# Two attentions and two gated layers on one core: where the first four weight units are loaded and converted

## The chip, the cores and the metric

The kernel runs on one core of one Trainium2 chip. The metric is device time of one execution in microseconds (us), lower is better. The engines named below are TensorE (PE, with its weight loads shown as PEld), VectorE (DVE), ScalarE (ACT), GpSimd (POOL) and SyncE (SP, which here only issues DMAs).

## The reference, cut to what matters

Four batches of 576 tokens. Attention runs per batch with 8 heads of 64 columns: scores, a threshold at the row maximum minus `tau`, exponentials of what is above it, division by their sum, times `v`. The four results, side by side as 2304 rows of 512, then pass two layers of the same shape:

```python
h = x @ w_in                       # 512 -> 2048
g = h * clip(h + 3, 0, 6) / 6      # layer 1; layer 2: g = max(h, 0)**2
x = g @ w_out                      # 2048 -> 512
```

Activations are f32 in and out.

## The kernel before, in words

**Attention.** A *unit* is one pair of heads of one batch (16 units, `u0` to `u15`), and a unit has nine *jobs* of 128 query rows (four of head 0, one for both tails, four of head 1). Batches 0 and 1 are jobs 0 to 71. `attention()` is a generator, and one *attention step* is one pass of the loop in `run` (line 457): `scores` and `soft1` of job i, `soft2` of job i-1, the product with v (`av`) of job i-5 (`LAG`), a bit of preparation of the next unit, and on three of nine jobs a load of k, q or v. A job's chain is: score matmuls on PE (L289), row minimum on DVE (L299), exponential on ACT (L309), threshold and sum on DVE (L316), cast to f16 on ACT (L322), the remainder on POOL (L323, L324), a transpose by DMA from SP's queue (L326), and the `av` matmuls (L348). Tiles of the job that matter here: the f16 pair p16 of a job in batches 0 and 1 is taken by `new_w("o")` (L318), so it sits in one of the **four `wpo` buffers** (`N_W = 4`), which are the buffers of converted `w_out` units. It is held from L322 until its transpose has landed. The products of `av`, the transposed results (`finish`, L365) and the small broadcast matmuls of `all_max` (L117) share two PSUM buffers (`ps_a`).

**Weights.** The weights come as f64 words. A *weight unit* is 256 of the 2048 hidden columns of `w_in`, or hidden rows of `w_out`: 1 MB in HBM. `wseq` lists them in order of use; numbers 0, 1 are the first `w_in` pair (kind i), 2, 3 the first `w_out` pair (kind o), 4, 5 i, 6, 7 o, and so on, 32 for both layers of batches 0 and 1. `w_load` brings one in (L538, L541) into one of three raw buffers (`wd`, `NWD = 3`). `group_scale` needs both units of a pair: a reduction of each on DVE (L557), `all_max` on PE (L117), a few small DVE operations. `w_next` then converts one unit into an exact f16 pair: ACT (L624), DVE (L627 and L628 for units 0 to 3; for later ones ACT L632 and DVE L633), the cast on ACT (L635) into a `wpi` or `wpo` buffer, the remainder on POOL (L636), and a store of the pair to a scratch in HBM from SP's queue (L638), from which batches 2 and 3 read it later.

**The layers.** The matmuls of the layers come in *steps* of 24 matmuls of 288 columns: a hidden step (`hidden`, L702: one of 16 blocks of 128 hidden columns of one batch) with its gate (ACT L706, DVE L707, ACT L712, POOL L713), and an output step (`output`, L742: one of four blocks of output columns over four hidden blocks). Both take their PSUM from the three `ps_s` buffers, which the attention scores also use. Segments alternate between batch 0 and batch 1; the order of steps at the start is: hidden 0 to 3 of batch 0 (steps 0 to 3), the first hidden step of batch 1 (step 4), four output steps of batch 0 (5 to 8), the other three hidden steps of batch 1 (9 to 11), the first hidden step of the next group (12). A weight unit serves two hidden blocks: step 0 needs unit 0, step 2 unit 1, step 5 units 2 and 3 (all four blocks are summed), step 12 unit 4, step 18 unit 5, step 21 units 6 and 7. Step 4 needs x of batch 1, so all of jobs 36 to 71 and `split_x(1)`.

**The order.** It is written out by hand at the end of the kernel. `attn_to(n)` runs the attention up to step n. Before: attention alone to step 50, convert unit 0 (`want_w(0)`), to 54, unit 1, to 58, unit 2, to 62, unit 3, to 64; then the layers start. Each layer step yields twice, and `paced` runs attention steps between these half steps: steps 64 to 77 over half steps 0 to 8 (`ways`), then the attention of batch 2 over half steps 8 to 232. `tick` converts unit k ahead of layer step 4k - 12 (`LEAD_J`), so unit 4 at step 4, 5 at 8, 6 at 12, 7 at 16. `most` caps how far raw loads run ahead. All this is program order; the framework then plans each engine's own order of issue from it, ahead of time, and may put an instruction that is ready ahead of earlier ones that are not.

Of the kernel before, what the change touches and what calls it, by code (L numbers as in the profile page):

```python
# [21 lines left out]

LAG = 5
LOADS = (2, 4, 6)
FIRST_W = (50, 54, 58, 62)
FIRST_LD = 64
AHEAD = 8
PRE = 6
LEAD_J = 12
LEAD = 8  # L30
# [7 lines left out]
def attention_moe_moe_kernel(  # L38
# [12 lines left out]
    nc = tc.nc  # L51
# [333 lines left out]
    def split_scaled(b, src, s):  # L385
        for c in range(NC):
            new_x(b, c)
            nc.scalar.activation(out=xh[b][c], in_=src[c], func=AF.Copy, scale=s)
            nc.vector.scalar_tensor_tensor(out=xl[b][c], in0=src[c], scalar=s, in1=xh[b][c], op0=ALU.mult, op1=ALU.subtract)

    def split_x(b):
        s = st.tile([P, 1], F32, name="sx", bufs=2)
        e = xe[b] = st.tile([P, 1], F32, name="ex", bufs=4)
        nc.vector.tensor_reduce(out=s, in_=vscs[b], axis=AX.X, op=ALU.min)
        nc.vector.reciprocal(out=e, in_=s)
        src = []
        for c in range(NC):
            if b < 2:
                src.append(x_st[b][:, c, :])
            else:  # L400
                t = me.tile([P, S], F32, name="xr", bufs=2)
                nc.sync.dma_start(out=t, in_=x_st[b][c])
                src.append(t)
        split_scaled(b, src, s)
# [94 lines left out]
    wseq = []  # L499
# [20 lines left out]
    w_hl = {}  # L520
    n_ld = [0]
    n_sp = [0]
    most = [len(FIRST_W)]
    w16s = {}
    scaled = {}

    def new_w(kind):
        return wt.tile([P, 2, UW], F16, tag=f"wp{kind}", name=f"wp{kind}", bufs=N_W)

    def w_load():  # L530

        k = n_ld[0]
        src, kind, u, layer, b = wseq[k]
        n_ld[0] += 1
        t = wt.tile([P, UW, 2], I32, name="wd", bufs=NWD)
        if kind == "i":
            v64 = src[:, u * UF:(u + 1) * UF].rearrange("(c p) f -> p c f", p=P).bitcast(I32)
            nc.sync.dma_start(out=t.rearrange("p (c f) t -> p c (f t)", c=NC), in_=v64)  # L538
        else:
            v64 = src[u * UF:(u + 1) * UF, :].rearrange("(a p) e -> p a e", p=P).bitcast(I32)  # L540
            nc.sync.dma_start(out=t.rearrange("p (a e) t -> p a (e t)", a=UC), in_=v64)  # L541
        w_raw[k] = t
# [47 lines left out]
    def norm_scale(q):  # L590

        n = NQ // UC
        a = ps_a.tile([P, 512], F32, tag="acc", name="gr")
        ops = [(u, j) for u in range(q * n, q * n + n) for j in range(UW // P)]
        for i, (u, j) in enumerate(ops):
            w = w_hl[wuse[(2, 0, "i", u)]][:, 0, j * P:j * P + P]
            nc.tensor.matmul(a[:, 0:P], lhsT=w, rhs=w, start=i == 0, stop=i == len(ops) - 1)
        am = st.tile([P, 1], F32, name="gm", bufs=2)
        nc.vector.tensor_reduce(out=am, in_=a[:, 0:P], axis=AX.X, op=ALU.max)
        nc.vector.tensor_scalar(out=am, in0=am, scalar1=2.0 ** -40, scalar2=None, op0=ALU.max)  # L600
        m = all_max(am, ident_g)
        c = slice(q, q + 1)
        unit_of(m, m)
        nc.vector.reciprocal(out=r_w[1][:, c], in_=m)
        nc.vector.tensor_scalar(out=a_w[1][:, c], in0=m, scalar1=e_w[1][:, c], scalar2=2.0 ** 21, op0=ALU.mult, op1=ALU.mult)

    def w_next():
        k = n_sp[0]
        n_sp[0] += 1
        src, kind, u, layer, b = wseq[k]  # L610
        if b:
            w = new_w(kind)
            nc.sync.dma_start(out=w, in_=w16s[(layer, kind, u)])
            w_hl[k] = w
            return
        while n_ld[0] <= k:
            w_load()
        if k == len(FIRST_W):
            with tc.issue_after(last_hp[0].ins):
                group_scale(k)  # L620
        sp = group_scale(k)
        d = w_raw.pop(k)
        c = t = wt.tile([P, UW], F32, name="wc", bufs=2)
        nc.scalar.activation(out=c, in_=d[:, :, 1].bitcast(F32), func=AF.Prelu, scale=sp, alpha=2.0 ** 32)  # L624
        ci = c.bitcast(I32)
        if k < FIRST_DVE:
            nc.vector.tensor_scalar(out=ci, in0=ci, scalar1=3, scalar2=None, op0=ALU.logical_shift_left)  # L627
            nc.vector.scalar_tensor_tensor(out=t.bitcast(I32), in0=d[:, :, 0], scalar=29, in1=ci, op0=ALU.logical_shift_right, op1=ALU.bitwise_or)  # L628
        else:

            d16 = d.rearrange("p f t -> p (f t)").bitcast(U16).rearrange("p (f t) -> p f t", t=4)
            nc.scalar.activation(out=d[:, :, 0], in_=d16[:, :, 1], func=AF.Copy, scale=2.0 ** -13, bias=-4095.5 / 8192)  # L632
            nc.vector.scalar_tensor_tensor(out=t.bitcast(I32), in0=ci, scalar=3, in1=d[:, :, 0], op0=ALU.logical_shift_left, op1=ALU.bitwise_or)  # L633
        w = new_w(kind)
        nc.scalar.activation(out=w[:, 0], in_=t, func=AF.Copy)  # L635
        nc.gpsimd.tensor_tensor(out=w[:, 1], in0=t, in1=w[:, 0], op=ALU.subtract)  # L636
        dr = scr.tile([P, 2, UW], F16, name=f"scr{k}")
        nc.sync.dma_start(out=dr, in_=w)  # L638
        w16s[(layer, kind, u)] = dr
        w_hl[k] = w  # L640
        while n_ld[0] < len(wseq) and wseq[n_ld[0]][4] == 0 and n_ld[0] < most[0] and len(w_raw) < NWD:
            w_load()
        n = NQ // UC
        if layer == 2 and kind == "i" and u % n == n - 1:
            norm_scale(u // n)
        if k + 1 < min(len(wseq), most[0]) and wseq[k + 1][4] == 0 and wseq[k + 1][2] % n == 0:
            group_scale(k + 1)

    def want_w(k):
        while n_sp[0] <= k:  # L650
            w_next()

    def tick(step):
        while n_sp[0] < len(wseq):
            k = n_sp[0]
            if (4 * k - LEAD_J if k < n_j else 4 * n_j + 2 * (k - n_j) - LEAD) > step:
                break
            w_next()

# [7 lines left out]
    def stepped():  # L667
        tick(gstep[0])
        gstep[0] += 1
# [143 lines left out]
    segs = []  # L813
# [13 lines left out]
    n_j = 2 * 2 * NF // UC  # L827
# [4 lines left out]
    def attn_to(n):  # L832
        while steps[0] < n:
            if next(gen, None) is None:
                return
            steps[0] += 1

    for i, n in enumerate(FIRST_W):
        attn_to(n)
        want_w(i)  # L840
    attn_to(FIRST_LD)
    most[0] = len(wseq)

    jobs_b = 9 * NPAIR
    a1 = 2 * jobs_b + LAG
    a2 = a1 + PRE + jobs_b + LAG
    a3 = a1 + PRE + 2 * jobs_b + LAG
    split_x(0)
    ways = [(0, a1 - AHEAD - LAG), (8, a1), (2 * 116, a2), (2 * 150, a3)]
    done = {8: 1, 2 * 116: 2, 2 * 150: 3}  # L850
    hs = [0]

    def paced():
        for (g0, n0), (g1, n1) in zip(ways, ways[1:]):
            if g0 <= hs[0] <= g1:
                attn_to(n0 + math.ceil((n1 - n0) * (hs[0] - g0) / (g1 - g0)))
        if hs[0] in done:
            split_x(done[hs[0]])

    def go(steps_):  # L860
        for _ in steps_:
            hs[0] += 1
            paced()

    paced()
    for i, g in enumerate(segs):
        f0 = g.q * NQ
        for f in range(f0 + (1 if i else 0), f0 + NQ):
            go(hidden(g, f))
        if i + 1 < len(segs):  # L870
            go(hidden(segs[i + 1], segs[i + 1].q * NQ))
        go(output(g))

# [29 lines left out]
```

## Time and profile before

| | us |
|---|---|
| three timed runs | 1101.16, 1103.22, 1103.37 |
| their median | 1103.22 |
| the profiled execution | 1103.31 |
| its span, first to last instruction | 1101.5 |
| TensorE busy in that span | 1024.0 |
| VectorE, ScalarE, GpSimd busy | 618.8, 646.5, 503.9 |

The profiled execution took 1.8 us more than its span (what lies around the instructions), and 0.09 us more than the median of the runs. All times within the profile are counted from the first instruction. A share of busy time over the whole span mixes three stages: attention alone (to about 170 us), layers with attention beside them (to about 760), layers alone.

### The profile page before, as it was taken

How to read it: one execution, taken by the hardware profiler on the slowest of the kernel's cores; microseconds unless marked ns; L12 is line 12 of the kernel's file. 1: busy time of each engine (PE TensorE's matmuls, PEld its weight loads, DVE VectorE, ACT ScalarE, POOL GpSimd, SP SyncE). 2: the span in 40 equal slices, each digit the busy share in tenths (PEclk: the TensorE clock that was granted, in tenths of full speed). 3: DMA queues.
4: the chain of work that ended last, by engine and by line, in shares of the span. 5: the costliest groups of instructions: out<-in, count | busy, mean ns of one | idle time of the engine just before them, and what ended most of it. 6: DMA issues, size and time to landing. Idle time of an engine off the chain costs nothing.

```text
span 1101.5 us, 23226 instructions
## 1 busy us (share of the span) xinstructions
PE 1024.0 (93%) x9232; PEld 820.2 (74%) x9232; DVE 618.8 (56%) x1286; ACT 646.5 (59%) x1118; POOL 503.9 (46%) x665
## 2 busy tenths in 40 slices
PE   6888857899899998999999999999999999999998
PEld 4756645777687787778778787788887778778776
DVE  5877886467846678665665676654451232222122
ACT  6988977689746657785766567774433224223322
POOL 6877866555745445454555345554222111222111
PEclk9998988999999999999999999999999999999999
DMA  9998998476936536565545566766322233233211
GB/s 247 193 186 159 173 239 195 76 237 188 247 78 162 166 85 190 119 186 142 161 126 127 147 135 122 173 150 158 120 97 77 77 96 110 82 96 120 78 39 43
DMA packets 255820, 154.34 MB, mean 140 GB/s; under 512 B 215520, under 2 KB 227808, under 8 KB 255712
## 3 DMA queue, kind: packets, MB, share of 16 engines
q1 hardware_dynamic: 254064, 152.34, 55.7%
q8 instruction: 72, 1.18, 0.4%
q10 hardware_dynamic: 1648, 0.52, 0.3%
q14 instruction: 36, 0.29, 0.1%
HBM read 84.15 MB, written 23.86 MB: 98 GB/s over the span
## 4 chain that ended last, share of the span: by engine, by line
PE 58%; DMA 14%; DVE 11%; ACT 8%; issue 4%; POOL 4%; SPq 0%; POOLq 0%; ACTq 0%; DVEq 0%
PE y L742 27%; PE hp L702 22%; DMA wd<-in_moe_w_in_dram 4%; DMA wd<-in_moe_w_out_dram 3%; DMA vraw<-in_v_dram 3%; PE o L348 2%; DVE wc L633 2%; PE s L293 2%; DMA pt<-wpo 2%; PE s L289 2%; ACT wc L624 1%; ACT wpo L322 1%; DVE nm L299 1%; POOL wpo L324 1%; ACT g L309 1%
## 5 line engine op out<-in xcount | busy, mean ns | idle before, releaser
L702 PE MATMUL hp<-x,wpi 128*128 128x288 f16 x3072 | 396.2, 287 | 8.3 <-DVE g L707 2.5
L702 PEld LDWEIGHTS <-wpi 128*128 128x128 f16 x3072 | 298.9, 98 | 85.5 <-issue 9.5
L742 PEld LDWEIGHTS <-wpo 128*128 128x128 f16 x3072 | 297.4, 98 | 83.7 <-issue 6.0
L742 PE MATMUL y<-gh,wpo 128*128 128x288 f16 x2048 | 334.1, 286 | 8.3 <-DVE g L710 3.3
L713 POOL TENSOR_TENSOR gl<-g,gh 128x576 f16<-128x576 f32 x128 | 164.7, 1289 | 334.2 <-ACT gh L712 332.1
L742 PE MATMUL y<-gl,wpo 128*128 128x288 f16 x1024 | 207.3, 286 | 0.3 <-POOL gl L713 0.3
L748 DVE SCALAR_TENSOR_TENSOR ya<-y,yq,ya 128x576 f32<-128x576 f32 (+1 forms) x97 | 78.3, 810 | 108.3 <-PE y L742 107.7
L712 ACT ACTIVATE gh<-g 128x576 f16<-128x576 f32 x128 | 86.9, 679 | 61.4 <-DVE g L710 33.8
L299 DVE TENSOR_REDUCE nm<-s 128x1 f32<-128x576 f32 x144 | 107.7, 750 | 25.0 <-PE s L293 16.3
L289 PE MATMUL s<-kf,q_pl 128*128 128x288 f32 x288 | 94.2, 457 | 17.4 <-DVE g L316 14.1
L348 PE MATMUL o<-v,pt 128*128 128x64 f16 (+1 forms) x2016 | 88.4, 198 | 15.8 <-DMA pt<-wpo 5.4
L348 PEld LDWEIGHTS <-pt 128*128 128x128 f16 x2016 | 79.2, 99 | 31.4 <-issue 13.2
L709 ACT ACTIVATE g<-hp,r_w 128x576 f32<-128x576 f32 x64 | 47.0, 735 | 91.7 <-PE hp L702 91.5
L710 DVE TENSOR_TENSOR g<-g,hp 128x576 f32<-128x576 f32 x64 | 48.0, 751 | 85.8 <-ACT g L709 85.8
L706 ACT ACTIVATE g<-hp,r_h,aq 128x576 f32<-128x576 f32 x64 | 52.8, 826 | 62.4 <-PE hp L702 60.6
L707 DVE SCALAR_TENSOR_TENSOR g<-g,r_w,hp 128x576 f32<-128x576 f32 x64 | 51.8, 810 | 60.3 <-ACT g L706 60.1
L324 POOL TENSOR_TENSOR p<-e,p 128x512 f16<-128x512 f32 x72 | 84.5, 1173 | 0.0
L324 POOL TENSOR_TENSOR wpo<-g,wpo 128x512 f16<-128x512 f32 x72 | 84.0, 1166 | 0.0
L289 PEld LDWEIGHTS s<-kf,q_pl 128*128 128x128 f32 x288 | 54.7, 209 | 32.7 <-issue 11.3
L316 DVE SCALAR_TENSOR_TENSOR e<-s,thr,e 128x576 f32<-128x576 f32 x72 | 58.5, 815 | 27.3 <-ACT e L309 26.0
L322 ACT ACTIVATE p<-e 128x576 f16<-128x576 f32 x72 | 49.0, 680 | 34.7 <-DVE e L316 23.6
L316 DVE SCALAR_TENSOR_TENSOR g<-s,thr,g 128x576 f32<-128x576 f32 x72 | 58.0, 810 | 15.6 <-ACT g L309 12.8
(129 smaller groups left out, 1169.5 us busy)
## 6 DMA issues: line engine op xcount, KB each, us to landing
wd<-in_moe_w_in_dram SPq DMA_DIRECT2D x16, 1024.0 KB, 6.2
wd<-in_moe_w_out_dram SPq DMA_DIRECT2D x16, 1024.0 KB, 6.4
wpi<-scr SPq DMA_DIRECT2D x32, 512.0 KB, 3.9
wpo<-scr SPq DMA_DIRECT2D x32, 512.0 KB, 4.0
scr<-wpi SPq DMA_DIRECT2D x16, 512.0 KB, 5.7
scr<-wpo SPq DMA_DIRECT2D x16, 512.0 KB, 5.4
kraw<-in_k_dram SPq DMA_DIRECT2D x16, 256.0 KB, 4.3
vraw<-in_v_dram SPq DMA_DIRECT2D x16, 256.0 KB, 3.7
```

Source lines behind the costliest of these rows:

```text
L289: nc.tensor.matmul(s[:, half, 0:HALF], lhsT=u.qf[:, t, :], rhs=u.kf[:, c], start=True, stop=True)
L299: nc.vector.tensor_reduce(out=j.nm, in_=j.s, axis=AX.XY, op=ALU.min)
L316: nc.vector.scalar_tensor_tensor(out=j.e, in0=j.s, scalar=j.thr, in1=j.e, op0=ALU.is_le, op1=ALU.mult, accum_out=u.sm[:, col:col + 1])
L322: nc.scalar.activation(out=p16[:, 0:S], in_=e, func=AF.Copy)
L324: nc.gpsimd.tensor_tensor(out=p16[:, S + TAIL:], in0=e[:, 0:NT * P], in1=p16[:, 0:NT * P], op=ALU.subtract)
L348: nc.tensor.matmul(o[:, n * w:n * w + w], lhsT=j.pt[:, c, :], rhs=vv[:, hs, vc, :], start=i == 0, stop=i == len(ops) - 1)
L702: last_hp[0] = nc.tensor.matmul(hp[:, a, 0:HALF], lhsT=wsl(seg, "i", f, w, c), rhs=x[c][:, a * HALF:(a + 1) * HALF], start=i == 0, stop=i ...
L706: nc.scalar.activation(out=g, in_=hv, func=AF.Relu, bias=r_h[:, q:q + 1], scale=seg.aq)
L712: nc.scalar.activation(out=gh, in_=gf, func=AF.Copy)
L713: nc.gpsimd.tensor_tensor(out=gl, in0=gf, in1=gh, op=ALU.subtract)
L742: nc.tensor.matmul(a[:, k_, 0:HALF], lhsT=wsl(seg, "o", f, w, e), rhs=g[f][:, k_ * HALF:(k_ + 1) * HALF], start=i == 0, stop=i == len(ops) ...
L748: nc.vector.scalar_tensor_tensor(out=y, in0=av_, scalar=yq, in1=y, op0=ALU.mult, op1=ALU.add)
```

## The change

- The four conversions leave the attention of batches 0 and 1. The attention runs alone to step 62, three `w_load` are called there, it runs on to step 70, unit 0 is converted, to step 72, unit 1, and the layers start at step 73.
- Units 2 to 7 get due steps of their own (`EARLY`): units 2 and 3 at layer steps 0 and 1, unit 4 at 5, 5 at 9, 6 at 11, 7 at 13. From unit 8 on the old rule holds.
- Attention steps 73 to 77 are spread over half steps 0 to 4 instead of 64 to 77 over 0 to 8; `split_x(1)` follows at half step 4 instead of 8, and batch 2's attention is spread over half steps 4 to 232.
- Units 0 to 3 are not stored to the scratch when they are converted; each is stored behind the store of unit 4, 5, 6 or 7.
- The cap on raw loads is lifted at half step 4, with two explicit `w_load` at half step 6.

```diff
-FIRST_W = (50, 54, 58, 62)
-FIRST_LD = 64
-AHEAD = 8
+FIRST_LD = 62
+FIRST_W = (70, 72)
+FIRST_MM = 73
+EARLY = {2: 0, 3: 1, 4: 5, 5: 9, 6: 11, 7: 13}
+N_FIRST = 4
...
-    most = [len(FIRST_W)]
+    most = [N_FIRST]
+    late_st = []
...
-        if k == len(FIRST_W):
+        if k == N_FIRST:
             with tc.issue_after(last_hp[0].ins):
                 group_scale(k)
...
-        nc.sync.dma_start(out=dr, in_=w)
+        if k < N_FIRST:
+            late_st.append((dr, w))
+        else:
+            nc.sync.dma_start(out=dr, in_=w)
+            if late_st:
+                a, c = late_st.pop(0)
+                nc.sync.dma_start(out=a, in_=c)
...
-            if (4 * k - LEAD_J if k < n_j else 4 * n_j + 2 * (k - n_j) - LEAD) > step:
+            if EARLY.get(k, 4 * k - LEAD_J if k < n_j else 4 * n_j + 2 * (k - n_j) - LEAD) > step:
...
+    attn_to(FIRST_LD)
+    w_load()
+    w_load()
+    w_load()
     for i, n in enumerate(FIRST_W):
         attn_to(n)
         want_w(i)
-    attn_to(FIRST_LD)
-    most[0] = len(wseq)
...
-    ways = [(0, a1 - AHEAD - LAG), (8, a1), (2 * 116, a2), (2 * 150, a3)]
-    done = {8: 1, 2 * 116: 2, 2 * 150: 3}
+    ways = [(0, FIRST_MM), (4, a1), (2 * 116, a2), (2 * 150, a3)]
+    done = {4: 1, 2 * 116: 2, 2 * 150: 3}
...
+        if hs[0] == 6:
+            w_load()
+            w_load()
         if hs[0] in done:
             split_x(done[hs[0]])
+            most[0] = len(wseq)
...
-        if i + 1 < len(segs):
+        if i < len(segs) - 1:
```

## Rows read from the trace of the kernel before

**Rows 1.** The page: PE over the span, and its busy tenths in 40 slices.
```profile
PE 1024.0 (93%) x9232; PEld 820.2 (74%) x9232; DVE 618.8 (56%) x1286; ACT 646.5 (59%) x1118; POOL 503.9 (46%) x665
...
PE   6888857899899998999999999999999999999998
```

**Rows 2.** Windows: stretch, its us, busy us of PE PEld DVE ACT POOL, clock, DMA.
```profile
94.00:125.00 31.00, 25.78 (x301) 19.89 (x299) 26.34 (x60) 28.44 (x64) 24.98 (x50) 1.00 0.96 171
...
151.00:161.00 10.00, 6.98 (x78) 5.19 (x77) 8.37 (x20) 7.94 (x16) 3.23 (x11) 1.00 0.83 215
161.00:171.50 10.50, 6.74 (x54) 4.95 (x55) 5.70 (x18) 9.98 (x21) 6.86 (x10) 0.51 0.94 268
171.50:213.50 42.00, 34.18 (x385) 26.41 (x384) 22.96 (x44) 29.05 (x57) 27.58 (x44) 1.00 0.69 133
...
225.00:325.00 100.00, 93.36 (x776) 73.83 (x775) 71.09 (x143) 73.90 (x108) 57.03 (x52) 0.98 0.69 200
```

**Rows 3.** Line L326 (transposes) in three stretches: count, ns min/median/max, first to last start.
```profile
L326 SPq DMA_TRANSPOSE pt<-wpo x19: 1258/1301/2347, 93.5 to 134.0; - x19
...
L326 SPq DMA_TRANSPOSE pt<-wpo x22: 1242/1298/4019, 134.0 to 210.3; - x22
...
L326 SPq DMA_TRANSPOSE pt<-wpo x8: 1258/1294/1534, 84.4 to 104.1; - x8
```

**Rows 4.** Line L322 (cast) from 171 to 214: what ACT's idle time awaited (us, times).
```profile
  DMA pt<-wpo: 8.4, 10
```

**Rows 5.** The chain that ended last, 170 to 214: start us, us, what.
```profile
198.31 3.19 DMA pt<-wpo
...
203.85 3.97 DMA pt<-wpo
```

**Rows 6.** Timeline of PE: start us, us, line, tiles, count [idle before].
```profile
129.90 0.57 PE L348 MATMUL o<-v,pt 128*128 128x64 f16 x14 [0.47 <-ACT os L355]
...
134.38 0.46 PE L117 MATMUL vm<-ident_m,gm 128*128 128x128 f32 x2 [1.01 <-ACT xr L378]
...
171.43 1.05 PE L702 MATMUL hp<-x,wpi 128*128 128x288 f16 x7
```

**Rows 7.** Conversion lines from 130 to 180, and one of them on POOL's timeline.
```profile
L624 ACT ACTIVATE wc<-wd,sp x4: 1221/1234/1247, 137.3 to 157.7; 128x1024 f32<-128x1024 f32 x4
...
L628 DVE SCALAR_TENSOR_TENSOR wc<-wd,wc x4: 1212/1216/1218, 140.3 to 160.7; 128x1024 int32<-128x1024 int32 x4
...
145.05 2.13 POOL L636 TENSOR_TENSOR wpi<-wc,wpi 128x1024 f16<-128x1024 f32 x1
...
L636 POOL TENSOR_TENSOR wpo<-wc,wpo x2: 2122/2123/2124, 162.7 to 176.9; 128x1024 f16<-128x1024 f32 x2
```

**Rows 8.** SP's timeline (raw loads), and landing times of L541's three loads before 180.
```profile
11.17 2.20 SPq L538 DMA_DIRECT2D wd<-in_moe_w_in_dram  x2
13.42 0.51 SPq L541 DMA_DIRECT2D wd<-in_moe_w_out_dram  x1
...
141.59 0.48 SPq L541 DMA_DIRECT2D wd<-in_moe_w_out_dram  x1
...
DMA to landing us min/median/max: 5.4/8.5/10.0
```

**Rows 9.** Timeline of PE: one full hidden step, and the end of step 8.
```profile
203.14 3.10 PE L702 MATMUL hp<-x,wpi 128*128 128x288 f16 x24
...
224.45 0.41 PE L742 MATMUL y<-gl,wpo 128*128 128x288 f16 x2
```

**Rows 10.** Windows at a lowered clock (columns as in rows 2).
```profile
297.80:301.20 3.40, 3.40 (x16) 2.13 (x15) 3.40 (x6) 2.83 (x5) 3.40 (x2) 0.50 1.02 362
```

**Rows 11.** The page's groups: gate of a step on ACT (busy, mean ns, idle).
```profile
L706 ACT ACTIVATE g<-hp,r_h,aq 128x576 f32<-128x576 f32 x64 | 52.8, 826 | 62.4 <-PE hp L702 60.6
...
L712 ACT ACTIVATE gh<-g 128x576 f16<-128x576 f32 x128 | 86.9, 679 | 61.4 <-DVE g L710 33.8
```

**Rows 12.** Timeline of DVE: a reduction that waited for its load.
```profile
166.32 1.22 DVE L557 TENSOR_REDUCE g<-wd 128x1 f32<-128x1024 f32 x1 [4.41 <-DMA wd<-in_moe_w_in_dram]
```

## The prediction, made before the changed kernel was run

> **What bounds the kernel now.** I read the page first, then windows, then single lines. The page gives PE 93% of the span [rows 1], and its slices say where the rest is: nines from about 210 us on, sixes to eights before. So what is to be had lies in the first 215 us, and from there on the kernel is as long as PE's work. The windows say what that early stage is. From 94 to 125 us, attention alone, no engine is free: PE 25.78 of 31, ACT 28.44, DVE 26.34 and a DMA share of 0.96 [rows 2]. There it makes 18 intervals between job transposes in 40.5 us, 2.25 us per job. From 134.0 on, where conversions and the first layer steps are mixed in, 21 intervals take 76.3 us, 3.63 per job [rows 3]. PE isn't the reason: it is busy 34.18 of 42 us from 171.5 to 213.5 [rows 2]. ACT's cast of a job waits ten times, 8.4 us in all, for an earlier transpose to land [rows 4], and the chain of the end runs through those transposes (3.19 and 3.97 us, two of several) [rows 5]. This is a shortage of buffers: the cast writes a `wpo` buffer, and once units 2 and 3 have been converted they hold two of the four.
>
> The mark for the sum is the end of step 8 (the fourth output step): 224.45 + 0.41 = **224.9 us** [rows 9]. There both attentions and nine steps are done, before and after alike, and PE is dense behind it: 93.36 of 100 us from 225 to 325 [rows 2]. What the change gains at this mark it keeps, unless that stretch becomes worse.
>
> **Part 1: what leaves the attention.** Four conversions, two of the `wpo` buffers, four stores, and the loads of units 3 to 6. The loads of units 0 to 2 don't move: they were issued at 11.17 and 13.42 us [rows 8], though the program has them at step 50; the three new `w_load` at step 62 will go as early, and I cost them at nothing. With the cover gone they would still have the 60 jobs before their use. Jobs 50 to 71 then keep the pace of attention alone: 134.0 + 21 x 2.25 = 181.3 for the last transpose instead of 210.3. That is **29.0 us earlier**, the gross gain.
>
> **Part 2: what becomes late.** The first layer step ran at 171.43 [rows 6]; now it waits for unit 0, whose chain begins with `all_max`. In before it stood 4.5 us behind an av block at 129.9, at 134.38, the time of job 50's transpose [rows 3, 6]. Twenty jobs later these are 129.9 + 45 = 174.9 and 179.4; with 0.57 for the block, the chain begins between 175.5 and 179.4. From there to the end of the first remainder (145.05 + 2.13) it took 12.8 us [rows 6, 7], among five jobs' soft operations. Its bare pieces that I have as rows are 0.46 + 1.23 + 1.22 + 2.13 = 5.0 [rows 6, 7]. So step 0 starts between 175.5 + 5.0 = 180.5 and 179.4 + 12.8 = 192.2. The nearest row is the whole chain; from the early end it gives 188.3, and the last jobs' soft work is nearly through by then. I take **187**. Unit 1 is wanted two attention steps later and two layer steps later; one POOL pass of 2.13 behind unit 0 is early enough, 0.
>
> **Part 3: nine steps without attention.** One step is 3.10 us [rows 9]; nine are 27.9. Two av blocks (0.57 each [rows 6]) and the last transposes on PE: 2. `split_x(1)` needs jobs that end before 187 and is wanted at step 4, 12 us later: 0.
>
> [...] At the low level 16 layer matmuls took 3.40 us, 0.21 each [rows 10], against 3.10/24 = 0.13: 39% of such a stretch is lost. Stretches of 3.4 and 10.5 us [rows 2, 10] give 1.3 and 4.1; if the clock holds, 0. I take 2. [...]
>
> Units 2 and 3: unit 3's load needs the raw buffer of unit 0. In before it was issued at 141.59, 7.2 us after `all_max` [rows 6, 8], so now at about 182.7 (counted from 175.5). It lands 5.4 to 8.5 us later [rows 8], 1.2 of reduction [rows 12], then a chain of 11.5 (what I took in part 2): unit 2 is ready at 201 to 204, unit 3 a POOL pass later, 203 to 206. Step 5 wants them from 187 + 5 x 3.10 + 2 = 204.5 on, the second half step later. This is what is late next; I take 1 us. Its ACT and DVE work is hidden by the steps: a step asks ACT for 0.83 + 0.68 of 3.10 us [rows 11], a conversion asks for 1.23 of ACT and a cast, 1.22 of DVE and a shift [rows 7].
>
> **Part 4: the rest.** The four stores now stand behind those of units 4 to 7, on SP's queue, with nothing to wait for; they come into a stretch with a DMA share of 0.69 [rows 2]. Units 4 and 5 are due one step later, 6 and 7 one and three steps earlier. Batch 2's attention starts two steps earlier in the layers' count. All this falls on 225 to 325 us, where DVE and ACT are busy 71 and 74 of 100 and PE idles 6.6. That idle time bounds a gain; a loss I bound by a wait like DVE's 4.41 for a load [rows 12]. I take 0. The last line of the diff does nothing.
>
> **The sum.** 187 + 27.9 + 2 + 2 + 1 = 219.9, against 224.9: **5.0 us earlier**. The profiled execution took 1103.3 (span 1101.5 plus 1.8, and within 0.1 of the median), so 1098.3. Of the gross 29.0 us, 15.6 go to the later step 0 (171.4 to 187), and most of the rest to steps that before were done beside the jobs. About 0.2%, 2.2 us, can be told from no change.
>
> **Rivals.**
> *Larger gain.* The chain shrinks towards its bare pieces, as the engines empty. Step 0 at 180.5, no clock loss, no wait: 180.5 + 27.9 + 2 = 210.4, 14.5 us earlier, 1088.8. For it: 7.8 of the 12.8 us lie outside those pieces, among the work of jobs. Against: small DVE operations between the pieces aren't in the 5.0.
>
> *No change.* Attention alone isn't always at 2.25: eight transposes from 84.4 to 104.1 took 2.8 us per interval [rows 3]. One unit of nine jobs at that pace costs 9 x 0.55 = 5, and takes the whole gain: 1103. One uncovered 4.41 us wait leads to 1102.7 as well. [...]
>
> *Slower.* The first `w_out` pair becomes the bound. In before its two remainders were 162.7 and 176.9, 14.2 us apart [rows 7], with ACT busy 9.98 of 10.5 [rows 2]. With the same gap unit 3 is ready at 202.7 + 14.2 + 2.1 = 219, and the 3.5 steps that are left take 10.9: 229.9, 5 us later, 1108.3; with step 0 at 192.2, 1113. It decides from unit 3 ready at 224.9 - 10.9 = 214. Against: no job then needs `wpo` buffers, and ACT has room.
>
> *The change doesn't do what it says:* units 2 and 3 could be put ahead of the last casts and take the buffers again, as loads were put ahead. Their scale needs unit 3's load, which needs unit 0 converted, at 182 or later, when the last cast is over. I give it nothing.
>
> **Chances.** Forecast (2.2 to 10 us faster) 0.44; larger gain 0.18; no change 0.15; slower 0.23. So faster 0.62. Low: 180.5 and an idle us of the next stretch back, 1088. High: step 0 at 192.2, 4.1 for the clock and 5 for the `w_out` pair or a load give 192.2 + 27.9 + 2 + 4.1 + 5 = 231.2, 6.3 later: 1110.
>
> **What would show it.** Right: 22 transposes from job 50 on at about 2.25 us, the last near 181; no cast waiting for a landing; first hidden step near 187, end of step 8 near 220, the stretch behind it as dense as now. Wrong: a first step behind 192; PE idle ahead of step 5 for unit 2 or 3; DVE or ACT waiting for raw loads while PE idles between steps 5 and 25; or a pace of jobs that stays above 3, which would mean that the buffers were not what held them.

## The result, and the profile after

| | before | changed |
|---|---|---|
| median of the timed runs, us | 1103.3 | 1089.42 (1083.89 to 1091.22) |
| profiled execution, us | 1103.31 | 1089.70 |
| its span | 1101.5 | 1087.9 |
| last transpose of batches 0 and 1 issued | 210.3 | 178.8 |
| first hidden step (step 0) | 171.4 | 181.0 |
| end of step 8 (the prediction's mark) | 224.9 | 218.9 |
| hidden step 36 starts | 447.2 | 440.3 |
| output step 64 starts | 714.6 | 701.0 |

The changed kernel takes 0.9869 of the time before, 95% interval 0.9831 to 0.9907: faster, by some 14 us (1.3%). (Steps 36 and 64 are counted from 0, among hidden and among output steps.) The table says where: of the 13.6 us between the two spans, 6.0 are there at the mark (224.9 - 218.9), 6.9 at hidden step 36, and all 13.6 at output step 64. So the gain was made at two places, half of it where no row of the prediction had put any.

The page of the changed kernel, its PE line and slices, against [rows 1]: PE is busy 3.2 us less with the same 9232 matmuls, and the slices hardly differ. A gain of 1.3% made at two places isn't found on this view.

```profile
PE 1020.8 (94%) x9232; PEld 817.9 (75%) x9232; DVE 620.9 (57%) x1286; ACT 645.5 (59%) x1118; POOL 503.5 (46%) x665
...
PE   6988886899999998999999999999999999999998
```

Its transposes from job 50 to job 71 (columns as in [rows 3]): 21 intervals in 45.8 us, 2.18 per job instead of 3.63.

```profile
L328 SPq DMA_TRANSPOSE pt<-wpo x22: 1242/1331/2422, 133.0 to 178.8; - x22
```

Its windows (columns as in [rows 2]): the stretch of those jobs, the clock's fall ahead of step 0, and the stretch behind the mark. The granted clock is 0.50 from 176.4 to 186.7 and 1.00 on both sides of it (from 175.0 to 176.4 and from 186.7 to 190.0); PE had 19 instructions in those 10.3 us.

```profile
134.00:180.00 46.00, 32.72 (x386) 24.83 (x384) 39.90 (x96) 39.60 (x86) 37.95 (x71) 0.96 0.94 168
...
176.40:186.70 10.30, 4.72 (x19) 2.42 (x20) 6.36 (x7) 3.83 (x4) 7.15 (x5) 0.50 0.88 231
225.00:325.00 100.00, 94.05 (x819) 75.35 (x818) 73.18 (x157) 79.47 (x117) 57.67 (x53) 1.00 0.70 199
```

Its timeline of PE around step 0 (columns as in [rows 6]): `all_max`, the wait for unit 0's cast, the first matmuls (which need only the high half, so they don't wait for the remainder), output step 5's wait for unit 3, and the end of step 8.

```profile
172.99 0.46 PE L119 MATMUL vm<-ident_m,gm 128*128 128x128 f32 x2 [0.30 <-ACT os L357]
173.83 1.13 PE L350 MATMUL o<-v,pt 128*128 128x64 f16 x28 [0.38 <-DVE mx L121]
181.03 1.14 PE L711 MATMUL hp<-x,wpi 128*128 128x288 f16 x4 [6.07 <-ACT wpi L638]
182.89 0.66 PE L711 MATMUL hp<-x,wpi 128*128 128x288 f16 x2 [0.72 <-ACT wpi L638]
183.78 4.99 PE L711 MATMUL hp<-x,wpi 128*128 128x288 f16 x28 [0.23 <-POOL wpi L639]
...
205.29 0.42 PE L751 MATMUL y<-gh,wpo 128*128 128x288 f16 x2 [0.18 <-POOL wpo L639]
...
218.47 0.41 PE L751 MATMUL y<-gl,wpo 128*128 128x288 f16 x2
```

Its timeline of POOL, the remainders of units 0 and 1, of unit 2 and of unit 3:

```profile
181.05 4.75 POOL L639 TENSOR_TENSOR wpi<-wc,wpi 128x1024 f16<-128x1024 f32 x2 [2.25 <-ACT wpi L638]
...
198.97 2.92 POOL L639 TENSOR_TENSOR wpo<-wc,wpo 128x1024 f16<-128x1024 f32 x1 [3.37 <-issue]
...
203.10 2.14 POOL L639 TENSOR_TENSOR wpo<-wc,wpo 128x1024 f16<-128x1024 f32 x1
```

Its timeline of SP: units 3 and 4 are loaded behind the last transposes, and the stores (L647).

```profile
180.23 0.53 SPq L544 DMA_DIRECT2D wd<-in_moe_w_out_dram  x1
181.82 0.37 SPq L541 DMA_DIRECT2D wd<-in_moe_w_in_dram  x1
183.75 2.42 SPq L647 DMA_DIRECT2D scr<-wpi  x2
...
201.92 3.68 SPq L647 DMA_DIRECT2D scr<-wpo  x2
```

The four stores that the code puts behind units 4 to 7 are issued right behind their own conversions, and the three loads written at step 62 are issued at 10.5 to 12.7 us. The framework put them ahead, as it did with the loads in before [rows 8].

### The profile page after: what moved, and what is told of

It is laid out like the page before. It is cut to its first block, busy times and chain, and to the rows that moved or that the text cites. A ratio compares the mean times of both kernels' runs of the same rounds, so it can differ in the third digit from the quotient of the medians.

```text
span 1087.9 us, 23244 instructions
## 1 busy us (share of the span) xinstructions
PE 1020.8 (94%) x9232; PEld 817.9 (75%) x9232; DVE 620.9 (57%) x1286; ACT 645.5 (59%) x1118; POOL 503.5 (46%) x665
## 4 chain that ended last, share of the span: by engine, by line
PE 63%; DVE 10%; ACT 10%; DMA 10%; issue 4%; POOL 3%; SPq 0%; POOLq 0%; ACTq 0%; DVEq 0%
PE y L751 29%; PE hp L711 26%; DMA wd<-in_moe_w_out_dram 4%; DMA wd<-in_moe_w_in_dram 3%; PE s L295 3%; PE o L350 2%; DMA vraw<-in_v_dram 2%; ACT g L311 2%; DVE wc L636 2%; DVE nm L301 2%; ACT wpo L324 2%; PE s L291 1%; DVE g L318 1%; ACT wc L627 1%; POOL wpo L326 1%
## 5 line engine op out<-in xcount | busy, mean ns | idle before, releaser
L291 PE MATMUL s<-kf,q_pl 128*128 128x288 f32 x288 | 91.9, 447 | 12.9 <-DVE g L318 10.6
L326 POOL TENSOR_TENSOR p<-e,p 128x512 f16<-128x512 f32 x72 | 85.0, 1180 | 0.0
L326 POOL TENSOR_TENSOR wpo<-g,wpo 128x512 f16<-128x512 f32 x72 | 84.4, 1172 | 0.0
L318 DVE SCALAR_TENSOR_TENSOR e<-s,thr,e 128x576 f32<-128x576 f32 x72 | 58.4, 814 | 28.5 <-ACT e L311 27.9
L318 DVE SCALAR_TENSOR_TENSOR g<-s,thr,g 128x576 f32<-128x576 f32 x72 | 58.0, 810 | 12.0 <-ACT g L311 10.5
```

The source lines that it names most:

```text
L291: nc.tensor.matmul(s[:, half, 0:HALF], lhsT=u.qf[:, t, :], rhs=u.kf[:, c], start=True, stop=True)
L318: nc.vector.scalar_tensor_tensor(out=j.e, in0=j.s, scalar=j.thr, in1=j.e, op0=ALU.is_le, op1=ALU.mult, accum_out=u.sm[:, col:col + 1])
L326: nc.gpsimd.tensor_tensor(out=p16[:, S + TAIL:], in0=e[:, 0:NT * P], in1=p16[:, 0:NT * P], op=ALU.subtract)
```

## The experiments

Two questions were open: what sped the jobs up (buffers, conversions, or the weights' DMA), and where the 6.6 us behind step 36 came from. Medians of before moved between 1099.8 and 1103.3 from one group of runs to the next, so ratios to the before beside each run are given.

**The buffers alone.** `o_pair_in_wpi` is before with one line changed; units 2 and 3 no longer take `wpo` buffers.

```diff
-        w = new_w(kind)
+        w = new_w("i" if k in (2, 3) else kind)
```

> The kernel before, with one edit: units 2 and 3, still converted behind attention steps 58 and 62, take wpi buffers instead of wpo buffers, so the jobs keep all four. Theory A (buffers: the jobs were slow because units 2 and 3 held two of the four wpo buffers): jobs 50 to 71 run at 2.6 us or less, the last transpose starts near 190 instead of 210.3, no cast waits for a landing, end of step 8 near 212, about 1092 us. Theory B (work: the conversions, their loads and stores slowed the jobs on DVE, ACT, POOL and DMA): the jobs stay above 3.2 us, the last transpose is at 203 or later, 1099 to 1103 us.

Ratio 0.9941 (0.9915 to 0.9968). The cast waits for no landing any more (8.4 us before, 0.0 now), the mark is at 215.9, but jobs take 3.15 us, between the two theories:

```profile
L326 SPq DMA_TRANSPOSE pt<-wpo x22: 1241/1301/4949, 133.9 to 200.1; - x22
```

That is 10 of the 30.5 us between 3.63 and 2.18 (21 intervals of 0.48). The shortage was real, and a third of the matter.

**The second pair late, the first left among the jobs.** `o_pair_late` is before with:

```diff
-FIRST_W = (50, 54, 58, 62)
+FIRST_W = (50, 54)
+EARLY = {2: 0, 3: 1}
+N_FIRST = 4
...
+            most[0] = len(wseq)
```

> The kernel before, with units 2 and 3 alone moved behind the attention (due at layer steps 0 and 1), units 0 and 1 still behind attention steps 50 and 54, the layers from step 64, stores at once. Theory A (buffers): the last transpose near 187, first layer step near 171 as before, so some steps run beside the last jobs; end of step 8 near 212, about 1090 us. Theory B (work): units 0 and 1 with their loads still slow the jobs to 2.9 us or more, last transpose near 195, about 1097 us.

Ratio 0.9923 (0.9901 to 0.9946). Jobs at 3.44, not at 2.25, with only 2.7 us of casts waiting. But the second pair didn't get behind the jobs: its remainders on POOL start at 169.5 and 186.1, and the last transpose is issued at 204.3.

```profile
L638 POOL TENSOR_TENSOR wpo<-wc,wpo x2: 2125/2127/2129, 169.5 to 186.1; 128x1024 f16<-128x1024 f32 x2
```

The mark is again at 215.9, 9.0 before that of before and 3.0 before that of the changed kernel; of these, 2.0 and 1.0 are there at job 50 already (132.0 against 134.0 and 133.0). And yet the whole is slower than the changed kernel: something behind the mark was missing here.

**The first pair early, the rest as changed.** `i_pair_early` is the changed kernel with:

```diff
-FIRST_W = (70, 72)
+FIRST_W = (50, 54)
...
-    attn_to(FIRST_LD)
-    w_load()
-    w_load()
-    w_load()
```

> The changed kernel, with units 0 and 1 converted behind attention steps 50 and 54 as before (they take no wpo buffer), everything else as changed: layers from step 73, units 2 and 3 at layer steps 0 and 1, stores late. In the changed kernel PE sits idle 6.1 us (175.0 to 181.0) ahead of the first layer step for unit 0, and the clock falls there. Theory A (buffers): that idle time and the clock go, the jobs stay at about 2.2 us, end of step 8 near 211 instead of 218.9, about 1082 us. Theory B (work): two conversions among the jobs cost them 5 us or more, which takes back what the first step gains: 1088 to 1091 us.

Ratio 0.9892 (0.9835 to 0.9949). Two conversions, with the loads that they set free, bring the jobs back to 3.00 us.

```profile
L328 SPq DMA_TRANSPOSE pt<-wpo x22: 1242/1613/4214, 132.4 to 195.4; - x22
```

**The same without the weights' DMA.** `i_early_loads_held` is that kernel with the loads and stores of weights tied behind the last job's transpose, in short:

```diff
-        nc.sync.dma_start_transpose(out=j.pt, in_=p16)
+        last_tr[0] = nc.sync.dma_start_transpose(out=j.pt, in_=p16)
...
+    attn_to(FIRST_MM)
+    with tc.issue_after(last_tr[0].ins):
+        w_load()
```

> The changed kernel with units 0 and 1 converted behind attention steps 50 and 54, as in i_pair_early, but with the raw loads of unit 3 and later, and the stores of units 0 to 3, ordered on SP's queue behind the transpose of the last job. So two conversions stay among the jobs and no weight DMA does. Theory E (DMA: the loads and stores took the DMA engines' time from the transposes): the last transpose is at 185 or earlier (i_pair_early 195.4, changed 178.8). Theory F (the conversions' work on DVE, ACT and POOL): it stays at 191 or later. End of step 8 under E: unit 3's load lands near 190, so step 5 waits until about 203, end near 216.

Ratio 0.9972 (0.9951 to 0.9993). Its three raw loads also moved to the very start of the program, ahead of the attention's own, and job 50 came at 138.8, 5.8 us later than in the changed kernel; so its time and its mark (226.1) aren't comparable, its pace is. The last transpose, at 191.8, would be that of theory F; less the 5.8 us it is 186.0, between E and F. The windows of the jobs' stretch, before first:

```profile
134.00:180.00 46.00, 31.03 (x299) 23.55 (x299) 35.97 (x88) 35.37 (x65) 29.23 (x48) 0.81 1.01 233
```

of `o_pair_in_wpi`:

```profile
134.00:180.00 46.00, 30.73 (x302) 23.17 (x303) 37.07 (x91) 38.49 (x70) 35.91 (x55) 0.93 1.08 242
```

of `i_pair_early`:

```profile
134.00:180.00 46.00, 30.39 (x286) 22.33 (x285) 38.81 (x90) 36.18 (x66) 31.62 (x54) 0.89 1.06 216
```

and of `i_early_loads_held`, from its job 50 on:

```profile
138.80:180.00 41.20, 32.80 (x345) 24.78 (x344) 33.59 (x84) 36.36 (x79) 33.07 (x57) 0.92 0.73 148
```

Read the last two columns, DMA share and GB/s (a packet counts where it starts, so the share of a window can pass 1): with weight transfers among the jobs more bytes move, at a DMA share above 1, while fewer jobs pass. Of `i_early_loads_held`, the transposes of jobs 50 to 71:

```profile
L328 SPq DMA_TRANSPOSE pt<-wpo x22: 1258/1308/1944, 138.8 to 191.8; - x22
```

53.0 us for 21 intervals: 2.52 per job with both conversions in and no weight transfer, against 3.00 with both (`i_pair_early`) and 2.18 with neither. So for the first pair the transfers cost 0.48 per job and the conversions' own work 0.34. What in a transfer costs this isn't shown. In `i_pair_early` the transposes of these jobs land later (median 4.2 us, longest 7.8, against 3.4 and 5.0 in `i_early_loads_held`), and four raw loads and two stores of weights stand between the transposes on SP's queue; the run took both away at once. In before, between 134 and 180 us, four raw loads (4 MB) and four stores (2 MB) shared the engines with 11 transposes; in the changed kernel 22 transposes pass in the same 46 us, at a share of 0.94.

**The late stores undone.** `stores_at_once` is the changed kernel with the plain store put back:

```diff
-        if k < N_FIRST:
-            late_st.append((dr, w))
...
+        nc.sync.dma_start(out=dr, in_=w)
```

> The changed kernel with the stores of units 0 to 3 issued at once instead of behind those of units 4 to 7. If the later stores matter: four 0.5 MB stores meet the raw loads of units 3 to 6 between 183 and 215 us, units 2 and 3 are later, end of step 8 at 221 or later, 1092 us. If they don't: the same as the changed kernel within the measurement, 1086 to 1091 us.

Ratio 0.9878 (0.983 to 0.9925), mark at 219.2: no difference, as the timeline of SP above says it must be.

**The last jobs and batch 2 at the old pace.** `split_at_8` is the changed kernel with:

```diff
-    ways = [(0, FIRST_MM), (4, a1), (2 * 116, a2), (2 * 150, a3)]
-    done = {4: 1, 2 * 116: 2, 2 * 150: 3}
+    ways = [(0, FIRST_MM), (8, a1), (2 * 116, a2), (2 * 150, a3)]
+    done = {8: 1, 2 * 116: 2, 2 * 150: 3}
```

> The changed kernel with the attention tail spread over half steps 0 to 8, split_x(1) at half step 8 and batch 2 spread over half steps 8 to 232, as before. Theory C (pace: between hidden steps 38 and 64 the changed kernel and its variants take 4 to 5 us less than the kernel before and its variants because batch 2's jobs stand at other places among the layer steps): the stretch from hidden step 38 to output step 64 goes back from 238.9 us to 242.5 or more, and the time rises to 1093 us or more. Theory D (it comes from the other due times, or from how far raw loads run ahead): that stretch stays below 240 us, the time at 1087 to 1091 us.

Ratio 0.9941 (0.9914 to 0.9968). The front is unharmed (mark at 219.1, step 36 at 438.3), and yet half of the gain is gone. From hidden step 36 to output step 64 it takes 266.7 us, where before takes 267.4 and the changed kernel 260.8 (from unrounded starts, here and below). This was the lead to the missing 6.6 us: spreading batch 2's attention over half steps 4 to 232 instead of 8 to 232 puts its jobs up to four half steps earlier.

**The old front with the new pace of batch 2.** `o_late_new_pace` is `o_pair_late` with the edit that `pace_alone` below has.

> The kernel before with only units 2 and 3 moved behind the attention, as in o_pair_late, and batch 2's attention on the changed kernel's line (half steps 4 to 232) from half step 9 on. Theory C (pace): it keeps o_pair_late's 8 to 12 us up to hidden step 36 and gains the 4 to 5 us of the later stretch as well: about 1085 us, better than both kernels. Theory D: 1090 to 1092 us, as o_pair_late.

Ratio 0.9909 (0.9883 to 0.9936). The stretch takes 260.7 us, so the pace came with it. The sum with `o_pair_late`'s mark did not: the mark is at 219.7 here and at 215.9 there, with the same order on every engine up to it, and no row says why; 2.2 of these 3.8 us are there at job 50 (134.2 against 132.0), 3.0 at step 0. Between the mark and step 36 it takes 224.3 us, against 219.4 in `o_pair_late`. So its profile loses ahead of step 36 what it gains behind it, and its timed runs gain next to nothing over `o_pair_late` (0.9909 against 0.9923): the time is that of theory D, the stretch that of C.

**The changed kernel a second time**, beside the last two:

> The changed kernel once more, on the chip of the two next runs and with more executions. If the gain is one of the order of work, its profile gives the same marks within 2 us (last job transpose 178.8, end of step 8 at 218.9, 260.8 us from hidden step 36 to output step 64) and the ratio stays between 0.983 and 0.991.

Ratio 0.9866 (0.9836 to 0.9897), last transpose at 180.0, mark at 217.6, the stretch 259.2: all as expected.

**Unit 0 earlier, so that PE doesn't wait for it.** `i_pair_at_64` changes two constants of the changed kernel (shown); `i_pair_at_62_spread_8` goes further and spreads the last jobs to half step 8, with batch 2's pace as changed.

```diff
-FIRST_W = (70, 72)
-FIRST_MM = 73
+FIRST_W = (64, 66)
+FIRST_MM = 67
```

> The changed kernel with units 0 and 1 converted behind attention steps 64 and 66 instead of 70 and 72, and the layers from step 67; steps 67 to 77 are spread over half steps 0 to 4. It aims at PE's idle 6.1 us ahead of step 0. If that wait is what is left at the front: step 0 starts near 171, its idle time goes, the last job transpose is at 183 or earlier, end of step 8 near 214, about 1085 us. If conversions and the load of unit 3 among the last jobs cost them as in i_pair_early (0.8 us per job over the last eight) and PE works beside them no faster: last transpose at 186 or later, end of step 8 at 217 to 219, no gain over the changed kernel.

> The changed kernel with units 0 and 1 converted behind attention steps 62 and 64, the layers from step 66, steps 66 to 77 spread over half steps 0 to 8 with split_x(1) at 8 as before, and batch 2 on the changed kernel's line from half step 9 on. If layer steps beside the last jobs are worth what o_pair_late showed (end of step 8 at 215.9): near 214, and with the new pace 1084 us. If the jobs' DMA and the conversions get in each other's way again: end of step 8 at 218 or later, 1089 us or more.

Ratios 0.9951 (0.9923 to 0.9979) and 0.9948 (0.9932 to 0.9965): both worse. Jobs slowed to 3.42 and 3.72 us each, the marks to 225.7 and 222.5, and the idle time ahead of step 0 that the first was to remove only moved. Its timeline of PE:

```profile
171.27 0.66 PE L711 MATMUL hp<-x,wpi 128*128 128x288 f16 x2 [5.11 <-ACT wpi L638]
```

**The pace alone.** `pace_alone` is before with nothing changed but batch 2's line, taken from half step 9 on:

```diff
-    ways = [(0, a1 - AHEAD - LAG), (8, a1), (2 * 116, a2), (2 * 150, a3)]
+    ways = [(0, a1 - AHEAD - LAG), (8, a1)]
+    later = [(4, a1), (2 * 116, a2), (2 * 150, a3)]
...
-        for (g0, n0), (g1, n1) in zip(ways, ways[1:]):
+        line = ways if hs[0] <= 8 else later
+        for (g0, n0), (g1, n1) in zip(line, line[1:]):
```

> The kernel before with one edit: from half step 9 on, batch 2's attention follows the changed kernel's line (half steps 4 to 232 instead of 8 to 232). Everything ahead of it is as before. Theory C (pace): up to the end of step 8 nothing changes (near 224.9, within 2 us); from hidden step 36 to output step 64 it takes 260 to 262 us instead of 267.5, and the time falls by 5 to 7 us, a ratio near 0.995. Theory D (the stretch depends on the due times of units 4 to 7 or on the loads): it stays at 266 us or more, the ratio at 0.999 to 1.001.

Ratio 0.994 (0.9911 to 0.9968), 6.6 us of the 1099.8 beside it, with jobs at 3.65 and the mark at 226.2, later than before's. The stretch takes 260.0. Over all profiles the stretch takes 258.9 to 260.8 us in the nine with the new line (the changed kernel, its repeat and seven others) and 266.7 to 269.7 in the four with the old one, whatever the front was.

What PE waits for in that stretch (line, releaser: us in total, times, longest), in before from 447.2 to 714.6:

```profile
PE y L742 <- DVE g L710: 3.3, 1, 3.3
PE y L742 <- DVE ya L748: 2.1, 1, 2.1
PE s L293 <- DVE e L316: 1.5, 1, 1.5
PE tps L178 <- ACT xr L378: 1.4, 1, 1.4
PE hp L702 <- ACT x L388: 1.3, 1, 1.3
```

in the changed kernel from 440.3 to 701.0:

```profile
PE y L751 <- DVE g L719: 2.6, 1, 2.6
PE s L295 <- DVE e L318: 1.5, 1, 1.5
PE ot L806 <- ACT xr L380: 0.5, 1, 0.5
```

in `split_at_8` from 438.3 to 705.0:

```profile
PE y L751 <- DVE g L719: 3.7, 1, 3.7
PE s L295 <- DVE e L318: 2.0, 2, 1.5
PE hp L711 <- ACT x L390: 1.3, 1, 1.3
PE y L751 <- DVE ya L757: 1.3, 1, 1.3
```

With the smaller rows these views add to 11.6, 5.5 and 11.1 us; `pace_alone`'s adds to 6.4. In each, one wait ended with the first instruction of the stretch and so lies ahead of it (1.3 us, `L702 <- ACT x L388`, in before; 1.3, 0.2 and 0.2 in `split_at_8`, the changed kernel and `pace_alone`). Without it they are 10.3, 5.4, 9.8 and 6.2. The windows of the same stretch, before first, then the changed kernel:

```profile
447.20:714.60 267.40, 257.00 (x2453) 212.03 (x2452) 170.68 (x371) 177.38 (x315) 132.52 (x154) 0.99 0.59 142
440.30:701.00 260.70, 255.30 (x2446) 210.91 (x2445) 168.18 (x368) 176.03 (x310) 134.19 (x156) 0.99 0.59 145
```

PE is idle for 10.4 us in the one and for 5.4 in the other, at the same granted clock. So 5.0 of the 6.7 us are waits of PE that vanish; the other 1.7 is PE's own busy time: seven matmuls (2453 against 2446) of batch 2's attention lie ahead of the stretch with the new line. Over all profiles these waits add to 9.8 to 11.0 us in the four with the old line and to 5.0 to 8.2 in the nine with the new one. One of them can be followed, the 2.1 us of `ya`: a wait of 1.3 to 2.3 us for `ya` stands in each of the four, and in none of the nine is there one of 0.4 or more. The timeline of DVE in before, where PE then resumes at 551.14 after 2.09 us:

```profile
548.28 1.22 DVE L557 TENSOR_REDUCE g<-wd 128x1 f32<-128x1024 f32 x1 [0.98 <-DMA wd<-in_moe_w_out_dram]
549.42 0.15 DVE L332 RECIPROCAL sm<-sm 128x1 f32<-128x1 f32 x1
549.60 0.76 DVE L299 TENSOR_REDUCE nm<-s 128x1 f32<-128x576 f32 x1
550.28 1.53 DVE L748 SCALAR_TENSOR_TENSOR ya<-y,yq,ya 128x576 f32<-128x576 f32 x2
```

The same place in the changed kernel:

```profile
537.98 0.80 DVE L757 SCALAR_TENSOR_TENSOR ya<-y,yq,ya 128x576 f32<-128x576 f32 x1
...
538.75 0.81 DVE L757 SCALAR_TENSOR_TENSOR ya<-y,yq,ya 128x576 f32<-128x576 f32 x1
539.48 0.75 DVE L301 TENSOR_REDUCE nm<-s 128x1 f32<-128x576 f32 x1
```

The additions `ya`, which free the PSUM buffer that PE's next output step needs, stood behind a weight reduction and a job's row minimum; now the row minimum comes behind them. (The reduction itself waited 0.98 us for its load.) Shown is that the new line removes these waits and that they carry most of the stretch's gain. Not shown is why this line hits better places than the old one; a line shifted otherwise wasn't tried.

## Why the prediction was right, and where not

1089.4 lies in the range, and the sign was forecast. The forecast itself, 1098.3, was 9 us too long, and the time is that of the rival "larger gain", but not by that rival's sum: its end of step 8 was 210.4, and the mark came at 218.9.

**Part 1, the pace of jobs: right, its cause incomplete.** 2.18 us per job against 2.25, last transpose at 178.8 against 181.3, casts waiting 0.5 us instead of 8.4. But "this is a shortage of buffers" names one of three things. Buffers alone gave 3.15; the rest is conversions on ACT, DVE and POOL and, for more than half of the first pair's share (0.48 against 0.34 per job), weight transfers between the transposes. The prediction had the row for it, a DMA share of 0.96 where attention ran alone [rows 2], and didn't use it.

**Part 2, step 0: too late by 6.0.** Forecast 187, 181.03 came, 0.5 behind the low end, 180.5. `all_max` stood at 172.99, not at 175.5 to 179.4: with jobs 1.0 us ahead at job 50 and 2.18 apart, the prediction's early end is 129.9 - 1.0 + 20 x 2.18 + 0.57 = 173.1, and it applies. And step 0 started on the high half of the weights when the cast was done, 8.0 us behind `all_max`, not at the end of the remainder (183.7, 10.7 behind it, against 12.8 in before).

**Part 3, the nine steps: too short by 5.0.** From step 0 to the mark 37.9 us instead of 32.9. The steps themselves need 27.9, as forecast. PE waited 3.7 where 1 was taken: 0.72 until the second cast was done and 0.23 for the first remainder, 1.3 until DVE had read an `all_max` product, 1.0 for a gate on ACT, the rest smaller. Other PE work takes what is left, some 3.9, instead of 2: five av blocks of 14 matmuls came behind step 0, not two. The clock was sized well: the 34 matmuls from 181.03 to 188.77 took 7.74 us, less 0.95 of idle and 34 x 3.10/24 = 4.39 at the pace of [rows 9], where the granted clock was 1.00, leaves 2.4, against 2. The granted clock fell from 1.00 to 0.50 (the prediction's low level [rows 10]) at 176.4, behind PE's last matmul at 175.0. In before it fell as well ahead of step 0, at 161, after ten us with PE busy 6.98 [rows 2], so the fall told nothing of the difference. What lowers the clock no run shows; the fall here lies 1.4 us into PE's 6.07 us of idle time.

The errors of parts 2 and 3 cancel: 5.0 us forecast at the mark, 6.0 measured, of which 1.0 was there already at job 50 (133.0 against 134.0), ahead of anything changed. That the forecast of the mark was so near is luck. And the time lies only 1.4 us inside the range, because of a gain that the prediction had put at 0 (part 4).

**The rivals at the front.** "Slower" by the `w_out` pair didn't come: the remainders ended at 201.9 and 205.2, 3.3 us apart instead of 14.2, and PE waited 0.18 for the second. "No change" by a late load didn't come either: PE's waits between steps 0 and 8 are those above, none longer than 1.3 behind the start. "The change doesn't do what it says" was given nothing, and in the form named there it didn't come. But two parts of the change do nothing: the three loads, as part 1 said, and the late stores, which part 4 took to stand behind those of units 4 to 7.

**Part 4, "the rest": the step that failed.** "Batch 2's attention starts two steps earlier in the layers' count ... I take 0", with a gain bounded by the 6.6 us of idle PE between 225 and 325. The change of line was seen, but its cost was sought in the next 100 us, and the gain arose from 440 to 715, where waits of PE add to 10.3 us. `pace_alone` measures it at 6.6 us (0.994). `split_at_8`, the change without it and without the closer spread of the last jobs, gives 0.9941. So the whole, 0.9869, is two nearly equal parts. It doesn't add to every front: in `o_late_new_pace` the stretch was as short, and the time fell by next to nothing.

A wait like DVE's 4.41 us for a load [rows 12] was the prediction's bound for a loss, and one way to "no change". What the DVE timelines show is 2.09 us of PE's time in before while `ya` stood behind a reduction, which had waited 0.98 us for its load, and a row minimum; here such a wait is what the change removes.

## What to carry to other kernels

Where two streams of work are interleaved by a formula over the whole kernel, a change of one end point moves every later item, so it is costed over all of that range, by PE's waits there, and measured by itself. Here the jobs paid 0.48 us each for the transfers of weights put among them, though no engine was busy there for more than 38.8 of 46 us (`i_pair_early`); see which transfers can move to a stage that has share to spare before counting buffers. Program order is no order of issue: look in the trace where a moved DMA went before giving the move a price.

## What wasn't expected

- Filling the idle 6.07 us ahead of step 0 by an earlier conversion costs more than it gives (0.9951 against 0.9866): jobs 50 to 71 then take 1.2 us more each (3.42 against 2.20).
- The jobs' stretch, with 22 transposes instead of 11, keeps PE hardly busier (32.72 against 31.03 us of 46, in before with layer steps from 171.4 on): the gain there is work of ACT and POOL (39.60 against 35.37, 37.95 against 29.23) that no longer waits.
- Two kernels with the same order of work up to the mark ended there 3.8 us apart (215.9 and 219.7). All but `i_early_loads_held` have the same order on every engine up to within 1 us of job 50's transpose, and it comes at 132.0 to 134.5 in them; so a difference of 2 us between two marks tells nothing by itself. The 13 profiles also differ by up to 5.7 us between the mark and step 36 (218.7 to 224.3). What makes this stays open. The two nearest versions, `stores_at_once` with 0.9878 and `i_pair_early` with 0.9892, can't be told from the changed kernel.
